# A six-layer cross network on one core: later loads, output copy, biases and first copies in another order, first tail weights loaded once

## The chip, the core and the metric

The kernel runs on one core of one Trainium2 chip. The metric is the device time of one execution in microseconds (us). The kernel before took 129.0 us (median of 3 runs, 128.87 to 129.28).

The engines are named as in the profile: PE (TensorE, matrix products, with its weight loads as PEld), DVE (VectorE), ACT (ScalarE), POOL (GpSimd) and SP (SyncE, which here only issues DMAs). ACT issues a few DMAs too. SBUF is the on-chip memory with 128 partitions, PSUM the banks into which PE writes.

## The reference

```python
B, F, D, L = 4096, 26, 16, 6          # Din = F * D = 416
x0: (4096, 416) bf16    ws: (6, 416, 416) bf16    bs: (6, 416) bf16

def reference(x0, ws, bs):
    x = x0
    for l in range(ws.shape[0]):
        x = x0 * (x @ ws[l] + bs[l]) + x
    return x
```

Every layer multiplies the current rows with a 416x416 matrix, adds a bias, multiplies by the first input elementwise and adds the current rows.

## The kernel before

**Form of the computation.** x after a layer is x0 times a sum, and the sum grows by one product and one bias per layer. So the sum stays in PSUM: PE adds each layer's product to it, and a layer ends when DVE adds the bias sum (`cb`) to the bank and multiplies by x0 (`leave`, L419). The bias sums of all layers are made once by `bias_sums` (L512): 16 small matmuls of `bsa_sb` (a row of ones, then the six bias rows; 7 partitions) with a 0/1 matrix `u_sb` (L265), copied to `cb_sb` by ACT.

**Tiling.** The 4096 rows are worked in NS = 4 blocks (s) of 1024 rows, each in two halves (h) of 512. Everything is held transposed, features in partitions: 416 = 3 chunks of 128 (c, k, m) and a tail of 32. The tails of the four groups of 256 rows lie in four quarters of 32 partitions (`quad(q)`). So the weights' tail rows `wt_sb` (32 rows of a layer) are wanted in all four quarters: `load_tail_weights` (L199) loads them four times from memory, once for each quarter, "wt0" for layer 0, "wt1" for layer 1, "wt2" for the rest. `corner` (L272, POOL) copies the last 32 columns of it into `wc_sb`.

**A layer (s, l).** On PE: the main products of half 0 (`main`, L312), then the tail rows for both halves (`tail_rows`, L328, in two functions `first` and `second`), then the tail's output columns (`tail_outs`, L370), then the main products of half 1. DVE leaves each bank. For the tail, ACT takes the two tail banks out of PSUM (`tail_halves`, L432), POOL multiplies by x0's tail (`leave_tail`, L441, the product at L449), and ACT and POOL make a swapped copy with two partition-shifted copies each (`swap`, L407, POOL's at L415). The next layer's tail rows wait for them. After each block but the last, `transpose_block` (L463) has SP issue three DMA transposes of the output chunks ("oT", L466) and one of the output tails ("ot", L471). `store_block` (L475) has POOL copy the transposed tails from `ot_sb` into `o_sb` (L477) and SP store the 1024 rows (L483); it is called for block s-1 in layer l = 1 of block s.

**Loads of x0.** The first half of block 0 comes as rows (`xin`, 2 x 208 KB, one on SP and one on ACT) and is transposed by PE (L497) into banks `HEAD_BANKS` and copied to `x0T_sb` by DVE (L506), six copies in the order (0,0), (1,0), (2,0), (0,1), (1,1), (2,1) of (chunk, part). All else comes by DMA transposes on SP: `load_transposed` (L203), and for the tails `load_last_columns` (L209), then `place_tail` (L215), six DMA copies within SBUF that wait for it. Block 0's tail comes from `xin` and `xtl` through PE (`tail_in`, L387) and ACT (L402).

**What sets the order.** `Plan.add` records each operation with what it reads and writes; each engine runs its operations in the order in which they were added, and waits are derived from the keys. `writes` replaces a key's writers, `parts` adds to them, `adds` is for accumulation. A POOL operation that shifts partitions (`shifts=True`) carries a key "shift". A queue's DMAs are issued in its engine's order too, so what waits on SP or ACT holds all that was added later.

In block 0, layer 0, PE's order is: `fill` (14 dummy matmuls, L285), the transposes, main products for k = 0, `bias_sums`, k = 1, `tail_in`, k = 2, `tail_rows`, `tail_outs`, half 1. The initial order of the DMA queues is at L229 to L249: SP issues xin0, three loads of layer 0's weights, the second half of block 0 transposed (x0T, L236), w1, wt1, w2, wt2, w3, w4, w5, and then for s = 1, 2, 3 the transposed loads, with `place_tail(1)` after block 1's, and last `xr` (the rows of block 3, for the end). ACT issues xin1, xtl, bs and the four copies of wt0.

The last layer of the last block is computed with rows in partitions (from L591) and is not touched.

Of the kernel before, what the change touches and what calls it, by code (L numbers as in the profile page):

```python
# [15 lines left out]
class Plan:  # L16
# [11 lines left out]
    def add(self, eng, fn, reads=(), writes=(), adds=(), parts=(), dma=None, shifts=False):  # L28
        if eng == "gpsimd" and dma is None:
            if shifts:  # L30
                adds = tuple(adds) + (("shift",),)
            else:
                reads = tuple(reads) + (("shift",),)
        op = Op()
        op.eng, op.fn, op.marked, op.dma, op.waits = eng, fn, False, dma, []
        needs = []
        for key in tuple(reads) + tuple(adds):
            needs += [(w, True) for w in self.writer.get(key, ())]
            if key[0] == "ps":
                needs += [(r, False) for r in self.readers.get(key, ())]  # L40
        for key in tuple(writes) + tuple(adds):
            needs += [(w, True) for w in self.writer.get(key, ())]
            needs += [(r, False) for r in self.readers.get(key, ())]
        for key in parts:
            needs += [(r, False) for r in self.readers.get(key, ())]
        clock = self.clock[eng]
        for need, raw in sorted(needs, key=lambda n: -n[0].idx):
            lane = need.group if need.dma else need.eng
            if dma and need.dma == dma:
                continue  # L50
            if need.dma is None and need.eng == eng and dma is None and (eng == "tensor" or not raw):
                continue
            if clock.get(lane, -1) >= need.idx:
                continue
            op.waits.append(need)
            need.marked = True
            for lane2, idx in need.clock.items():
                clock[lane2] = max(clock.get(lane2, -1), idx)
            clock[lane] = max(clock.get(lane, -1), need.idx)
        op.idx = len(self.ops[eng])  # L60
        op.group = None
        if dma:
            op.group = ("dma", dma)
            members = self.groups.setdefault(op.group, [])
            members.append(op)
            op.marked = True
        op.clock = dict(clock)
        self.ops[eng].append(op)
        for key in reads:
            self.readers.setdefault(key, []).append(op)  # L70
        for key in parts:
            if self.readers.get(key):
                self.writer[key], self.readers[key] = [], []
            self.writer.setdefault(key, []).append(op)
        for key in tuple(writes) + tuple(adds):
            old = self.writer.get(key, ())
            keep = [w for w in old if dma and w.dma == dma]
            self.writer[key] = keep + [op]
            if not keep:
                self.readers[key] = []  # L80
        return op
# [37 lines left out]
def bass_standalone__dcn_v2_cross__recsys_kernel(  # L119
# [6 lines left out]
    B, D = x0.shape  # L126
# [15 lines left out]
    with ExitStack() as es:  # L142

        def sb(name, shape, dt=BF16):
            return es.enter_context(nc.sbuf_tensor(name, shape, dt))
# [20 lines left out]
        ident = sb("ident", [128, 128])  # L166
        ones_sb = sb("ones_sb", [128, 128])
        dummy_sb = sb("dummy_sb", [128, 8])
        bsa_sb = sb("bsa_sb", [L + 1, D])
        u_sb = sb("u_sb", [L + 1, L])  # L170
        cb_sb = sb("cb_sb", [128, NC + 1, L], FP32)
        bt_sb = sb("bt_sb", [128, 1], FP32)
        ps = es.enter_context(nc.psum_tensor("ps", [128, 8, 512], FP32))
# [56 lines left out]
        load_rows("scalar", 1)  # L230
        for k in CH:
            load("sync", w_sb[:, 0, k, :], ws[0, 128 * k:128 * k + 128, :], "w0_%d" % k, [("w", 0, k)])
        load("scalar", xtl_sb[:, 4:JS, :], x0_v[:, 4:JS, DF:D], "xtl0", [("xtl", 0)])
        load("scalar", bsa_sb[1:L + 1, :], bs[:, :], "bs", [("bs",)])
        load_tail_weights(0, 1, "wt0", "scalar")
        load_transposed(0, H, SB)  # L236
        load_main(1)
        load_tail_weights(1, 2, "wt1")
# [2 lines left out]
        load_main(3)  # L241
        load_main(4)
        load_main(5)
        for s in range(1, NS):
            load_transposed(s, 0, SB)
            load_last_columns(s)
            if s == 1:
                place_tail(1)
        load("sync", xr_sb[:, :, :], x0_v[:, (NS - 1) * JS:NJ, :], "xr", [("xr",)])  # L249


        P.add("vector", lambda e: e.memset(ones_sb[:, :], 1.0), writes=[("ones",)])
# [7 lines left out]
                compare_op=ALU.is_equal, fill=0.0, base=0, channel_multiplier=1,  # L260
            ), reads=[("ones",)], writes=[("ident",)],
        )
        P.add("gpsimd", lambda e: e.memset(bsa_sb[0:1, :], 1.0), writes=[("bs1",)])
        P.add(
            "gpsimd", lambda e: e.affine_select(  # L265
                out=u_sb[:, :], in_=ones_sb[0:L + 1, 0:L], pattern=[[1, L]],
                compare_op=ALU.is_ge, fill=0.0, base=1, channel_multiplier=-1,
            ), reads=[("ones",)], writes=[("u",)],
        )
        P.add("gpsimd", lambda e: e.memset(wc_sb[:, :, :], 0.0), writes=[("wc", "wt%d" % i) for i in range(3)])  # L270

        def corner(a, b, name):  # L272
            P.add(
# [217 lines left out]
        for i in range(2):  # L491
            for c in CH:
                b = HEAD_BANKS[i][c]

                def fn(pe, i=i, c=c, b=b):
                    for j in range(2):
                        ins = pe.transpose(  # L497
                            out=psT[:, b, j * 128:(j + 1) * 128],
                            in_=xin_sb[:, 2 * i + j, c * 128:(c + 1) * 128], identity=ident[:, :],
                        )  # L500
                    return ins

                P.add("tensor", fn, reads=[("xin", i), ("ident",)], adds=[("ps", b)])
                dst, src = x0T_sb[:, c, i * 256:(i + 1) * 256], psT[:, b, 0:256]
                P.add(
                    "vector", lambda e, d=dst, s=src: e.tensor_copy(out=d, in_=s),  # L506
                    reads=[("ps", b)], writes=[("x0Tp", c, i)],
                )
        for c in CH:
            P.writer[("x0T", 0, c, 0)] = [w for i in range(2) for w in P.writer[("x0Tp", c, i)]]  # L510

# [17 lines left out]
            )  # L529


        corner(0, 1, "wt0")
        for s in range(NS):
            for l in range(L):
                ending = s == NS - 1 and l == L - 2
                if s == NS - 1 and l == L - 1:
                    break
                if s == 0 and l == 0:
                    for k in CH:
                        for part in range(2) if k == 0 else (None,):  # L540
                            for m in CH:
                                main(s, l, 0, m, k, part)
                        if k == 0:
                            bias_sums()
                        if k == 1:
                            tail_in()
                    tail_rows(s, l, True)
                    for c in CH:
                        leave(s, l, 0, c)
                    tail_outs(s, l, False)  # L550
                else:
                    for m in CH:
                        for k in CH:
                            main(s, l, 0, m, k)
                    tail_rows(s, l, l == 0)
                    for c in CH:
                        leave(s, l, 0, c)
                    tail_outs(s, l, False)
                if s == 0 and l == 1:
                    corner(2, L, "wt2")  # L560
                leave_tail(s, l, not ending)
                if l == 2 and 0 < s < NS - 1:
                    place_tail(s + 1)
                if s == 0 and l == 0:
                    corner(1, 2, "wt1")
                if l == 1 and s > 0:
                    store_block(s - 1)
                if ending:
                    P.add(
                        "gpsimd", lambda e: e.tensor_tensor(  # L570
                            out=bt_sb[:, :], in0=cb_sb[:, NC, L - 1:L], in1=cb_sb[:, NC, L - 2:L - 1], op=ALU.subtract
                        ), reads=[("cb",)], writes=[("bt",)],
                    )
                    P.add(
                        "gpsimd", lambda e, t=t32_sb[:, l % 2, :]: e.tensor_scalar_add(st_sb[:, :], t, bt_sb[:, :]),
                        reads=[("t32", l % 2), ("bt",)], writes=[("st",)],
                    )
                    for c in CH:
                        keep_sum(0, c, "scalar")
                for m in CH:  # L580
                    for k in CH:
                        main(s, l, 1, m, k)
                    leave(s, l, 1, m)
                if ending:
                    for c in CH:
                        keep_sum(1, c, ("scalar", "scalar", "vector")[c])
            if s < NS - 1:
                transpose_block(s)


        s, l = NS - 1, L - 1  # L591
# [128 lines left out]
```

## Time and profile before

| | us |
|---|---|
| runs, median of 3 | 129.0 (128.87 to 129.28) |
| profiled execution | 130.0 |
| its span, first to last instruction | 128.5 |
| PE busy | 123.2 |
| DVE busy | 98.5 |
| ACT busy | 43.5 |
| POOL busy | 37.4 |
| first main matmul, first tail matmul of layer 0 | 4.62, 8.52 |
| last matmul issued | 125.5 |

The granted PE clock was full (1.0) throughout. Matmuls are pipelined, and their ends are modelled, so a row's busy time is not its cost; what a stage costs is read from the starts of the same row in consecutive layers. "Idle before, releaser" in a row is how long the engine stood still before it and what ended that.

### The profile page before, as it was taken

What the parts mean: (1) busy time and instruction counts of PE and PEld (TensorE: products, weight loads), DVE (VectorE), ACT (ScalarE), POOL (GpSimd) and SP (SyncE); (2) the same over time, 40 slices, a digit from 0 to 9 for tenths busy, and PEclk for the clock granted to TensorE, in tenths of its full rate; (3) what the DMA queues carried; (4) which work ended last, traced back from release to release, by engine and by line L of the source; (5) the groups of instructions that cost most, each with busy time, mean ns of one, the idle gap of its engine ahead of it and who ended that gap; (6) DMA issues with size and microseconds to landing.
All of it is one profiled execution on the core that took longest, in us unless ns stands there. A gap on an engine that the chain in (4) does not pass through costs nothing.

```text
span 128.5 us, 5300 instructions
## 1 busy us (share of the span) xinstructions
PE 123.2 (96%) x2414; PEld 64.3 (50%) x2414; DVE 98.5 (77%) x152; ACT 43.5 (34%) x95; POOL 37.4 (29%) x79
## 2 busy tenths in 40 slices
PE   7979999999999999799999999999999999999991
PEld 5544554555545545345545545545555455455660
DVE  0329779779779779497797797797797797797973
ACT  0515225225205222343222252252222252253920
POOL 6005224134014040442221251241320351440550
PEclk9999999999999999999999999999999999999999
DMA  3998999013989894630009207200007706100017
GB/s 102 231 255 223 295 83 211 5 32 82 220 146 192 215 275 85 216 98 5 0 6 204 66 0 247 67 5 0 5 0 176 94 5 219 51 0 5 0 38 232
DMA packets 35059, 14.11 MB, mean 110 GB/s; under 512 B 25751, under 2 KB 35037, under 8 KB 35037
## 3 DMA queue, kind: packets, MB, share of 16 engines
q1 hardware_dynamic: 33744, 13.20, 48.5%
q10 hardware_dynamic: 1292, 0.57, 1.7%
q8 instruction: 19, 0.31, 1.1%
q14 instruction: 4, 0.02, 0.1%
HBM read 3.87 MB, written 3.41 MB: 57 GB/s over the span
## 4 chain that ended last, share of the span: by engine, by line
PE 83%; DMA 6%; DVE 4%; ACTq 2%; POOL 1%; issue 1%; SPq 0%
PE ps L280 83%; DMA wt_sb<-in_ws_dram 4%; DVE xT_sb L426 3%; DMA ot_sb<-xot_sb 3%; ACTq L189 2%; POOL xt_sb L415 1%; POOL xt_sb L449 0%; DVE o_sb L651 0%; SPq L466 0%; POOL o_sb L477 0%
## 5 line engine op out<-in xcount | busy, mean ns | idle before, releaser
L426 DVE SCALAR_TENSOR_TENSOR xT_sb<-ps,cb_sb,x0T_sb 128x512 bf16<-128x512 f32 x120 | 80.9, 743 | 20.2 <-PE ps L280 20.2
L280 PE MATMUL ps<-xT_sb,w_sb 128*32 128x512 bf16 (+1 forms) x1596 | 84.2, 364 | 0.0
L280 PEld LDWEIGHTS ps<-xT_sb,w_sb 128*32 128x32 bf16 x1596 | 40.9, 97 | 37.2 <-issue 4.0
L436 ACT ACTIVATE t_sb<-ps,cb_sb 64x256 f32<-64x256 f32 x46 | 21.6, 470 | 56.7 <-PE ps L280 56.4
L449 POOL TENSOR_TENSOR xt_sb<-t_sb,x0t_sb 128x256 bf16<-128x256 f32 x20 | 13.4, 672 | 59.2 <-ACT t_sb L436 59.2
L413 ACT ACTIVATE xt_sb<-xt_sb 32x256 bf16<-32x256 bf16 x38 | 15.7, 414 | 17.0 <-POOL xt_sb L449 16.7
L280 PE MATMUL ps<-x0T_sb,w_sb 128*32 128x512 bf16 (+1 forms) x348 | 18.8, 358 | 0.3 <-DVE x0T_sb L506 0.3
L415 POOL COPY xt_sb<-xt_sb 32x256 bf16<-32x256 bf16 x38 | 14.9, 393 | 2.4
L426 DVE SCALAR_TENSOR_TENSOR xo_sb<-ps,cb_sb,x0T_sb 128x512 bf16<-128x512 f32 x18 | 12.1, 742 | 2.5 <-PE ps L280 2.5
L280 PEld LDWEIGHTS ps<-x0T_sb,w_sb 128*32 128x32 bf16 x348 | 8.6, 97 | 7.8 <-issue 0.8
L280 PE MATMUL ps<-xt_sb,wt_sb 32*128 32x512 bf16 (+1 forms) x152 | 11.6, 326 | 0.8 <-POOL xt_sb L415 0.8
L280 PE MATMUL ps<-xt_sb,wc_sb 32*128 32x256 bf16 x76 | 7.3, 268 | 0.0
L280 PEld LDWEIGHTS ps<-xt_sb,wt_sb 32*128 32x128 bf16 x152 | 2.4, 91 | 8.9 <-DVE xT_sb L426 6.8
L280 PE MATMUL ps<-w_sb,xT_sb 128*32 128x416 bf16 (+1 forms) x60 | 5.1, 339 | 0.0
L449 POOL TENSOR_TENSOR xot_sb<-t_sb,x0t_sb 128x256 bf16<-128x256 f32 x3 | 2.0, 672 | 9.9 <-ACT t_sb L436 9.9
L651 DVE TENSOR_TENSOR o_sb<-ps,xr_sb 128x416 bf16<-128x416 f32 x6 | 3.4, 588 | 1.3 <-PE ps L280 1.0
L280 PEld LDWEIGHTS ps<-xt_sb,wc_sb 32*128 32x128 bf16 x76 | 3.9, 93 | 0.2
L288 PE MATMUL ps<-const-bfloat16-1.0 128*128 128x256 bf16 x14 | 3.1, 414 | 0.8 <-PEq L705 0.8
L506 DVE COPY x0T_sb<-ps 128x256 bf16<-128x256 bf16 x6 | 1.3, 282 | 3.1 <-PE ps L497 3.1
L280 PE MATMUL ps<-x0t_sb,wt_sb 32*128 32x512 bf16 (+1 forms) x32 | 2.4, 325 | 0.8 <-DMA wt_sb<-in_ws_dram 0.8
L458 ACT ACTIVATE sS_sb<-ps,cb_sb 128x512 bf16<-128x512 f32 x5 | 3.0, 691 | 0.0
L274 POOL COPY wc_sb<-wt_sb 128x32 bf16<-128x32 bf16 (+1 forms) x3 | 0.7, 237 | 7.7 <-DMA wt_sb<-in_ws_dram 7.6
(38 smaller groups left out, 26.7 us busy)
## 6 DMA issues: line engine op xcount, KB each, us to landing
out_dram<-o_sb SPq DMA_DIRECT2D x3, 832.0 KB, 4.2
w_sb<-in_ws_dram SPq DMA_DIRECT2D x5, 312.0 KB, 5.1
xr_sb<-in_x_dram SPq DMA_DIRECT2D x1, 832.0 KB, 6.4
wt_sb<-in_ws_dram SPq DMA_DIRECT2D x4, 104.0 KB, 3.5
out_dram<-o_sb SPq DMA_DIRECT2D x2, 208.0 KB, 2.2
w_sb<-in_ws_dram SPq DMA_DIRECT2D x3, 104.0 KB, 3.3
xin_sb<-in_x_dram ACTq DMA_DIRECT2D x1, 208.0 KB, 3.2
xin_sb<-in_x_dram SPq DMA_DIRECT2D x1, 208.0 KB, 3.0
```

The lines of the kernel that those rows point to most:

```text
L189: P.add(queue, lambda e: e.dma_start(dst, src), writes=writes, dma=name)
L274: "gpsimd", lambda e: e.tensor_copy(out=wc_sb[:, a:b, 3 * DR:4 * DR], in_=wt_sb[:, a:b, DF:D]),
L280: return pe.matmul(dst, lhsT=lhsT, rhs=rhs, start=start, stop=True, skip_group_check=True, tile_position=pos,)
L288: ins = pe.matmul(ps[:, 7, 0:256], lhsT=const[:, 0:128], rhs=const, start=True, stop=True)
L413: fn = lambda e, d=dst, s=src: e.activation(out=d, in_=s, func=ACTF.Copy)
L415: fn = lambda e, d=dst, s=src: e.tensor_copy(out=d, in_=s)
L426: "vector", lambda e: e.scalar_tensor_tensor(out=dst, in0=ps[:, bank(h, c), :], scalar=cb_sb[:, c, l:l + 1], in1=x0T_sb[:, c, o:o + H], op ...
L436: "scalar", lambda e, p=p, h=h: e.activation(out=dst[p, :], in_=ps[p, T_BANK[h], 0:G], func=ACTF.Identity, bias=cb_sb[p, NC, l:l + 1]), re ...
L449: "gpsimd", lambda e: e.tensor_tensor(out=dst, in0=t, in1=x0t_sb[:, s, 0, :], op=ALU.mult),
L458: fn = lambda e: e.activation(out=o, in_=i, func=ACTF.Identity, bias=b)
L506: "vector", lambda e, d=dst, s=src: e.tensor_copy(out=d, in_=s),
L651: "vector", lambda e: e.tensor_tensor(out=o_sb[:, jj, :], in0=ps[:, b, 0:D], in1=xr_sb[:, j, :], op=ALU.mult), reads=[("ps", b), ("xr",)], ...
```

## The change

Six edits:

1. wt0, the tail weights of layer 0, are loaded once, into the first quarter, as ACT's second DMA (before xtl). A new function `replicate`, called just before the first `corner`, copies them to the other quarters: to 1 and 2 by POOL, to 3 by ACT.
2. bs is loaded by a DMA that POOL issues, after DVE has cleared the whole of `bsa_sb`; DVE also writes the row of ones, which POOL did. `bsa_sb` and `u_sb` now have 128 partitions instead of 7.
3. `bias_sums` stands behind `tail_in` (after k = 1) instead of after k = 0.
4. DVE's six first copies are taken out of the transposes' loop and stand in the order (0,0), (1,0), (0,1), (2,0), (1,1), (2,1).
5. The transposed loads of blocks 2 and 3 and `xr` are no longer issued at the start, but behind the output transposes of blocks 0, 1 and 2.
6. `store_block(s-1)` is called in layer 3 of block s instead of layer 1.

One line in `Plan.add` makes a shifting POOL operation wait for the end of the POOL operations ahead of it, which before were only in order.

```diff
-            needs += [(r, False) for r in self.readers.get(key, ())]
+            needs += [(r, key == ("shift",)) for r in self.readers.get(key, ())]
...
-        bsa_sb = sb("bsa_sb", [L + 1, D])
-        u_sb = sb("u_sb", [L + 1, L])
+        bsa_sb = sb("bsa_sb", [128, D])
+        u_sb = sb("u_sb", [128, L])
...
+        load("scalar", wt_sb[quad(0), 0, :], ws[0, DF:D, :], "wt0", [("wtq",)])
         load("scalar", xtl_sb[:, 4:JS, :], x0_v[:, 4:JS, DF:D], "xtl0", [("xtl", 0)])
-        load("scalar", bsa_sb[1:L + 1, :], bs[:, :], "bs", [("bs",)])
-        load_tail_weights(0, 1, "wt0", "scalar")
...
-        for s in range(1, NS):
-            load_transposed(s, 0, SB)
-            load_last_columns(s)
-            if s == 1:
-                place_tail(1)
-        load("sync", xr_sb[:, :, :], x0_v[:, (NS - 1) * JS:NJ, :], "xr", [("xr",)])
+        load_transposed(1, 0, SB)
+        load_last_columns(1)
+        place_tail(1)
...
-        P.add("gpsimd", lambda e: e.memset(bsa_sb[0:1, :], 1.0), writes=[("bs1",)])
+        P.add("vector", lambda e: e.memset(bsa_sb[:, :], 0.0), writes=[("bs0",)])
+        P.add("vector", lambda e: e.memset(bsa_sb[0:1, :], 1.0), reads=[("bs0",)], writes=[("bs1",)])
+        P.add("gpsimd", lambda e: e.dma_start(bsa_sb[1:L + 1, :], bs[:, :]), reads=[("bs0",)], writes=[("bs",)], dma="bs")
...
+        def replicate():
+            for g, eng in ((1, "gpsimd"), (3, "scalar"), (2, "gpsimd")):
+                dst, src = wt_sb[quad(g), 0, :], wt_sb[quad(0), 0, :]
+                if eng == "scalar":
+                    fn = lambda e, d=dst, r=src: e.activation(out=d, in_=r, func=ACTF.Copy)
+                else:
+                    fn = lambda e, d=dst, r=src: e.tensor_copy(out=d, in_=r)
+                P.add(eng, fn, reads=[("wtq",)], parts=[("wt", "wt0")], shifts=True)
...
+        for c, i in ((0, 0), (1, 0), (0, 1), (2, 0), (1, 1), (2, 1)):
+            dst, src = x0T_sb[:, c, i * 256:(i + 1) * 256], psT[:, HEAD_BANKS[i][c], 0:256]
...
+        replicate()
         corner(0, 1, "wt0")
...
-                        if k == 0:
-                            bias_sums()
                         if k == 1:
                             tail_in()
+                            bias_sums()
...
-                if l == 1 and s > 0:
+                if l == 3 and s > 0:
                     store_block(s - 1)
...
             if s < NS - 1:
                 transpose_block(s)
+            if s < NS - 2:
+                load_transposed(s + 2, 0, SB)
+                load_last_columns(s + 2)
+            if s == NS - 2:
+                load("sync", xr_sb[:, :, :], x0_v[:, (NS - 1) * JS:NJ, :], "xr", [("xr",)])
```

More of the change, by code (lines that the diff above doesn't have):

```diff
@@ L262, in bass_standalone__dcn_v2_cross__recsys_kernel @@
         )
-        P.add("gpsimd", lambda e: e.memset(bsa_sb[0:1, :], 1.0), writes=[("bs1",)])
+        P.add("vector", lambda e: e.memset(bsa_sb[:, :], 0.0), writes=[("bs0",)])
+        P.add("vector", lambda e: e.memset(bsa_sb[0:1, :], 1.0), reads=[("bs0",)], writes=[("bs1",)])
+        P.add("gpsimd", lambda e: e.dma_start(bsa_sb[1:L + 1, :], bs[:, :]), reads=[("bs0",)], writes=[("bs",)], dma="bs")
         P.add(
             "gpsimd", lambda e: e.affine_select(
-                out=u_sb[:, :], in_=ones_sb[0:L + 1, 0:L], pattern=[[1, L]],
+                out=u_sb[:, :], in_=ones_sb[:, 0:L], pattern=[[1, L]],
                 compare_op=ALU.is_ge, fill=0.0, base=1, channel_multiplier=-1,
@@ L503, in bass_standalone__dcn_v2_cross__recsys_kernel @@
                 P.add("tensor", fn, reads=[("xin", i), ("ident",)], adds=[("ps", b)])
[L504 to L508, printed above, removed]
+        for c, i in ((0, 0), (1, 0), (0, 1), (2, 0), (1, 1), (2, 1)):
+            dst, src = x0T_sb[:, c, i * 256:(i + 1) * 256], psT[:, HEAD_BANKS[i][c], 0:256]
+            P.add(
+                "vector", lambda e, d=dst, s=src: e.tensor_copy(out=d, in_=s),
+                reads=[("ps", HEAD_BANKS[i][c])], writes=[("x0Tp", c, i)],
+            )
         for c in CH:
```

## The prediction

> **What bounds the kernel now.** I read the page's busy shares first, then the chain that ended last in order of time, then TensorE's instructions in order of time, then the waits and the DMA landings. The page, of the kernel before:
>
> ```profile
> span 128.5 us, 5300 instructions
> PE 123.2 (96%) x2414; PEld 64.3 (50%) x2414; DVE 98.5 (77%) x152; ACT 43.5 (34%) x95; POOL 37.4 (29%) x79
> ```
>
> TensorE is busy almost throughout, so only time in which TensorE stands still can be won. The chain in order of time (start, length, what) says where that is:
>
> ```profile
> 3.84 4.55 DMA wt_sb<-in_ws_dram
> 8.39 0.14 issue
> 8.52 34.59 PE ps L280 x648
> ...
> 47.81 3.31 DMA ot_sb<-xot_sb
> 51.12 0.05 issue
> 51.17 0.40 POOL o_sb L477
> 51.56 0.64 POOL xt_sb L449
> 52.21 0.05 issue
> 52.26 0.40 POOL xt_sb L415
> 52.66 0.05 issue
> 52.71 0.41 POOL xt_sb L415
> 53.12 0.14 issue
> 53.25 72.61 PE ps L280 x1388
> ```
>
> The reader is to see two foreign pieces between long TensorE pieces: the last of four loads of the first layer's tail weights, landing at 8.39, and a transpose of the output's tail (ot) for which GpSimd waits until 51.12. TensorE's own list shows what the second costs; these are the first tail matmuls of consecutive layers:
>
> ```profile
> 42.67 0.60 PE L280 MATMUL ps<-xt_sb,wt_sb 32*128 32x512 bf16 x7
> ...
> 47.55 0.60 PE L280 MATMUL ps<-xt_sb,wt_sb 32*128 32x512 bf16 x7
> ...
> 53.25 0.59 PE L280 MATMUL ps<-xt_sb,wt_sb 32*128 32x512 bf16 x7 [0.76 <-POOL xt_sb L415]
> ...
> 58.13 0.60 PE L280 MATMUL ps<-xt_sb,wt_sb 32*128 32x512 bf16 x7
> ```
>
> The step is 4.88 us from layer to layer (42.67 to 47.55, 53.25 to 58.13), but 5.70 from 47.55 to 53.25: 0.82 us lost. All other steps from 8.52 to 116.67 are 4.88, so nothing else stalls there.
>
> **The output copy, -0.82.** store_block(0) stands in layer l=1 of the next block; its copy (L477) heads GpSimd's queue and waits for ot:
>
> ```profile
> POOL o_sb L477 <- DMA ot_sb<-xot_sb: 4.8, 1, 4.8
> ```
>
> Queued behind it are the tail product (L449) and two swaps (L415), for which TensorE waits. The change moves the copy to l=3, about 10 us later, behind that layer's swaps. There it takes its 0.40 us (L477, 397 ns) out of GpSimd's idle stretch before the next product, 3.29 us in an ordinary layer (before 44.82). Without that cover it would cost at most 0.40 less the 1.15 us between the end of the swaps (41.52) and TensorE's need (42.67): nothing. Blocks 1 and 2 had no such wait (the row counts one), so the gain comes once. I take 0.82.
>
> On SP's queue the loads for blocks 2 and 3 and xr no longer stand ahead of block 0's output transposes: issues of 3.25 + 1.30 + 4.60 + 1.30 + 1.51 = 11.96 us (29.53 to 41.66). Before, oT0 was issued only at 41.70, though the DVE had its last tile by about 37.5; so ot should now land near 43, long before any copy asks. The price is later loads. x0T of block 2 would be issued near 41.5 and land 7.5 us later (the median of the four) near 49, for matmuls that begin at 65.84; its place_tail (six issues, 4.9 us) still ends before 60, for a use at 67.89. Block 3's come behind oT1 and ot1, which end at 71.49: land by about 80, x0t by 88, needed at 95 and 97. xr is issued near 101 behind ot2 and lands 6.4 us later, needed after 121. The output of block 0 leaves behind place_tail(2), that of block 2 about 114, landing 4.2 us later. Covers of 7 us and more: cost nothing.
>
> **The head.** Today first tail matmuls start at 8.52, 0.13 after the last wt0 landing; tail_outs start at 9.07. ScalarE issues wt0 as its fourth to seventh DMA (2.54 to 4.28). After the change one 26 KB copy is issued second, at about 1.30, where xtl stood, which landed 3.3 us later: at about 4.6. Then:
>
> - ScalarE no longer issues bs (0.66) and three wt0 (0.32 to 0.44 each), so its table load starts near 2.3, not 4.31; it is free at 3.8. Its 32x416 copy is bounded by a 32x256 copy (414 ns) and a 128x512 one (598): 0.53, done at 5.2, far from x0t at 6.9. Its tail input xtl is issued 0.45 later, lands near 5.1, needed at 6.5.
> - GpSimd does ident (to 1.42), the bs DMA (X), u (0.18), the clearing of wc (1.21), two copies, the corner (0.21). The copy goes by L415 (32x256, 393 ns) and L274 (128x32, 210 ns): 0.82 ns an element, so 0.52 at 416. With 0.1 for gaps the copies end at 1.42 + X + 0.18 + 1.21 + 1.04 + 0.10 = 3.95 + X. No row shows a DMA issued by GpSimd. [...] I take 0.66: done at 4.6, then held by wt0's landing to about 5.8.
> - The DVE's new clearing of bsa (like the 0.17 of L252) and the ones row (0.43 on GpSimd) end by 1.7; the DVE is idle to 4.17. Its reordered copies gain nothing: TensorE's pause at 5.31 is for bank 2, which holds the copy of (1,1), fifth in both orders.
> - bias_sums now follow tail_in. Their 16 matmuls (0.19 of TensorE's time, 5.86 to 6.05) change places, so k=2 starts at 6.93 as before and ends 0.64 later, 7.57; tail_in comes 0.19 earlier, so ScalarE's x0t ends at 7.57, not 7.76. With 128 rows in place of 7, weight loads may add 0.17 (x16 of 128x32 took 0.34, of 7x32 0.17), hidden by what follows.
>
> So tail matmuls could start at 7.65 and tail_outs 0.55 later, at 8.20, 0.87 before today. But tail_outs also read the transposed second half of block 0:
>
> ```profile
> x0T_sb<-in_x_dram SPq DMA_TRANSPOSE x1, 5.9
> ```
>
> Issued at 2.75, it lands at about 8.62. This is late next: 8.62 + 0.13 = 8.75. It may land sooner, since three of the four wt0 copies, 78 KB, leave the same engines; between 4.60 and 7.50 they carried 191 GB/s, so at most 0.42, at least 0. I take half, 0.21: tail_outs at 8.54, a gain of 0.53, with ends 0.32 and 0.87. The second layer's weights w1, issued at 4.88 and landing 4.5 later (9.4), are in time for 10.8.
>
> **Sum:** -0.82 - 0.53 = -1.35. The profiled execution took 130.0 us, its span 128.5, with 1.5 around it; the changed one should show a span of 127.1 and 128.6 in all. The runs' median, 129.0, is 1.0 below the profiled execution; the same difference gives 127.7.
>
> **Rivals.**
>
> *Only the GpSimd stall goes.* bs or the copies are late by just as much as wt0 was, or x0T binds later. For it: X and the landing of bs are in no row. Against it: bs is needed at 6.74, 5.3 us after its issue, and the loads issued in the first 4 us took 3.0 to 4.7, the transpose 5.9. Time: 129.0 - 0.82 = 128.2.
>
> *Only the head gains.* Executions without the profiler are 1.0 us shorter; if ot lands earlier in them, the stall is not there to be won. For it is that difference; against it, SP's loads ahead of ot fill its queue in any execution. 129.0 - 0.53 = 128.5.
>
> *Slower: GpSimd is held by its DMA.* Place: what stands behind bs in its queue, the wc clearing and the weight copies, for which the first tail matmuls wait. They start at 3.95 + X. Up to X = 4.0 it costs nothing (tail_outs wait for x0T until 8.54); at 4.57 the head's gain is gone; at 8.52 + 0.82 - 3.95 = 5.39 the whole gain. With the 6.99 of the longest issue row they start at 10.94, 2.42 late: 129.0 + 2.42 - 0.82 = 130.6. Against it: that row carries 1024 rows to transpose, bs six short ones.
>
> *Slower, by the bias wait.* If GpSimd's descriptors are not written before the DVE's six copies end (5.45) and bs needs xtl's 3.3 from there, it lands at 8.75; bias sums (0.13 + 0.19) and k=2 (0.64) put tail matmuls at 9.71, 1.19 late: 129.0 + 1.19 - 0.82 = 129.4. Against it: the DVE is idle from about 1.7 to 4.17, when GpSimd needs it to be. The Trainium skill ("SBUF — State Buffer", section "SBUF: two separate sides") has the rule behind this: a DMA issued by GpSimd has its descriptors written by GpSimd, which is locked out while the DVE runs a two-port fast mode. No row of this trace shows it.
>
> A fixed cost for DMAs issued by GpSimd stands in the Trainium skill ("DMA: Bandwidth & Descriptors", section "Anatomy of one DMA — SWDGE (gpsimd) path"): about 2.0 us, mostly completion. As an estimate by it bs would be there near 3.7, and the sum stays. No row here has it.
>
> **How the numbers follow.** Forecast 0.65; stall alone 0.14; head alone 0.10; GpSimd held 0.07; bias wait 0.04. A measurement of this kernel tells a difference from none at about 0.3%, 0.39 us: faster means below 128.6. The forecast and the stall alone are there, the head alone (128.5) so close to the bound that I give half of it: 0.84 faster; the other 0.05 and 0.02 for a GpSimd held by 5.0 to 5.8 make 0.07 the same; the rest, 0.09, is slower (X above 5.39 + 0.39 = 5.78, or the bias wait). The forecast's own range is 129.0 - 0.82 - 0.87 = 127.3 to 127.9 with the low gain; 0.3 below for what the x0T landing may add; up to 128.6 to hold both half gains: 127.0 to 128.6.
>
> **What would show it.** Right: layer steps of 4.88 throughout, with no wait of L477's copy; first tail matmuls near 7.7, then TensorE idle for x0T until about 8.5. Wrong: a TensorE wait for bs or for GpSimd's weight copies before the first tails, a GpSimd DMA of over 4 us, or a new wait for x0T, x0t or xr at 65, 95 or 121.

## The result, and the profile after

| | before | changed |
|---|---|---|
| median, us | 129.28 (15 runs, 128.87 to 129.97) | 128.62 (15 runs, 128.31 to 129.20) |
| ratio | | 0.9953, interval 0.9936 to 0.9971 |
| profiled execution, its span | 130.0, 128.5 | 129.03, 127.5 |

The change is faster: by 0.66 us of the medians (0.51%), by 0.47% in the ratio of the runs. The forecast was 127.7, a gain of 1.35 from a median of 129.0; the direction is right, the size about half, and the time lies just above the range. The kernel before took 129.28 in these 15 runs, so 0.28 of the distance to 127.7 lies in the median that the forecast set out from. The profiled executions differ by more than the medians, by 1.0: the 130.0 of the kernel before lies above all its 15 runs here, the 129.03 within those of the changed kernel. The page of the changed kernel begins:

```profile
span 127.5 us, 5305 instructions
PE 123.9 (97%) x2414; PEld 65.0 (51%) x2414; DVE 99.2 (78%) x154; ACT 44.0 (35%) x96; POOL 39.0 (31%) x81
```

Its chain that ended last, in order of time:

```profile
...
0.83 3.15 PE ps L295 x14
3.98 1.41 PE ps L504 x12
5.39 2.88 PE ps L287 x68
8.27 0.05 issue
8.32 116.51 PE ps L287 x2216
...
```

Both foreign pieces are gone: the chain is TensorE from the first dummy matmul on. TensorE's rows in order of time show the layers where the stall was:

```profile
47.34 0.60 PE L287 MATMUL ps<-xt_sb,wt_sb 32*128 32x512 bf16 x7
...
52.22 0.60 PE L287 MATMUL ps<-xt_sb,wt_sb 32*128 32x512 bf16 x7
...
57.10 0.60 PE L287 MATMUL ps<-xt_sb,wt_sb 32*128 32x512 bf16 x7
```

The steps are 4.88, and so are all others up to the last layer's at 115.64. The profiles thus differ by 0.82 in the stall and by only 0.20 in the head: the first tail matmuls went from 8.52 to 8.32, not to 7.65. Why shows in the timeline of the head. The kernel before:

```profile
3.81 0.89 PE L497 MATMUL ps<-ident,xin_sb 128*128 128x128 bf16 x12
...
7.16 0.60 ACT L402 ACTIVATE x0t_sb<-ps 128x512 bf16<-128x512 f32 x1 [0.77 <-PE ps L280]
...
8.52 0.59 PE L280 MATMUL ps<-x0t_sb,wt_sb 32*128 32x512 bf16 x7 [0.77 <-DMA wt_sb<-in_ws_dram]
```

The changed kernel:

```profile
1.58 0.75 POOL L261 DMA_DIRECT2D bsa_sb<-in_bs_dram  x1 [0.15 <-issue]
...
3.93 1.46 PE L504 MATMUL ps<-ident,xin_sb 128*128 128x128 bf16 x12
...
4.98 1.11 POOL L276 COPY wt_sb<-wt_sb 32x416 bf16<-32x416 bf16 x2 [1.27 <-DMA wt_sb<-in_ws_dram]
...
7.58 0.60 ACT L409 ACTIVATE x0t_sb<-ps 128x512 bf16<-128x512 f32 x1 [2.16 <-PE ps L287]
...
8.32 0.59 PE L287 MATMUL ps<-x0t_sb,wt_sb 32*128 32x512 bf16 x7
```

The same twelve transposes took 0.89 us in one execution and 1.46 in the other, a step of 0.055 against 0.106 us: TensorE ran at half speed in the second. The first full-speed record of the granted clock stands at 3.93 in the trace of before and at 6.37 in that of the changed kernel. Most executions of the kernel before hardly feel this, since its head ends with a DMA (in a2 below, which has the same head, the two stand level at a clock of 5.95); the head of the changed one is paced by TensorE.

### The profile page after: what moved, and what is told of

Same layout as the page of the kernel before. It is cut to its first block, busy times and chain, and to the rows that moved or that the text cites. A ratio compares the mean times of both kernels' runs of the same rounds, so it can differ in the third digit from the quotient of the medians.

```text
span 127.5 us, 5305 instructions
## 1 busy us (share of the span) xinstructions
PE 123.9 (97%) x2414; PEld 65.0 (51%) x2414; DVE 99.2 (78%) x154; ACT 44.0 (35%) x96; POOL 39.0 (31%) x81
## 4 chain that ended last, share of the span: by engine, by line
PE 97%; DVE 0%; issue 0%
PE ps L287 94%; PE ps L295 2%; PE ps L504 1%; DVE o_sb L664 0%
## 5 line engine op out<-in xcount | busy, mean ns | idle before, releaser
L287 PEld LDWEIGHTS ps<-w_sb,xT_sb 128*32 128x32 bf16 (+1 forms) x60 | 2.3, 97 | 1.4 <-issue 0.2
L675 POOL TENSOR_TENSOR o_sb<-f_sb,xr_sb 128x416 bf16<-128x416 f32 x2 | 1.9, 974 | 2.9 <-ACT f_sb L671 2.9
```

What stands on the lines that cost most here:

```text
L287: return pe.matmul(dst, lhsT=lhsT, rhs=rhs, start=start, stop=True, skip_group_check=True, tile_position=pos,)
L675: "gpsimd", lambda e: e.tensor_tensor(out=o_sb[:, jj, :], in0=t, in1=xr_sb[:, j, :], op=ALU.mult),
```

## The experiments

Ratios are to the kernel before on the same chip. In the table of heads (one profile each, us), "clock" is the first full-speed record of the granted clock in the trace (that of d2 holds none), "wt0" the last landing of the tail weights, "x0t" the end of ScalarE's copy, "k=2" the start of TensorE's last products before the tails, "x0T" the landing of block 0's second half, "tails" the first tail matmul.

| kernel | ratio | clock | wt0 | x0t | k=2 | x0T | tails |
|---|---|---|---|---|---|---|---|
| before, first profile | | 3.93 | 8.39 | 7.75 | 6.93 | 8.62 | 8.52 |
| a1 before again | 1.0016 | 5.51 | 8.31 | 7.98 | 7.16 | 8.52 | 8.44 |
| a2 edit 6 alone | 0.9985 | 5.95 | 8.18 | 8.20 | 7.37 | 8.40 | 8.32 |
| a4 edits 5, 6 | 0.9983 | 5.47 | 8.22 | 7.96 | 7.14 | 8.45 | 8.36 |
| changed, first profile | 0.9953 | 6.37 | 4.84 | 8.17 | 7.46 | 7.86 | 8.32 |
| b1 changed again | 0.9953 | 5.01 | 4.58 | 7.75 | 7.04 | 7.53 | 7.90 |
| d4 changed again | 0.9946 | 5.43 | 4.69 | 7.84 | 7.12 | 7.80 | 7.98 |
| a3 edits 1 to 4 | 0.9927 | 4.52 | 4.48 | 7.67 | 6.95 | 7.52 | 7.81 |
| b2 edits 1 to 4 again | 0.9971 | 5.79 | 4.88 | 7.91 | 7.19 | 7.70 | 8.05 |
| c1 edit 1 alone | 0.9989 | 5.53 | 4.49 | 8.37 | 7.55 | 7.67 | 8.43 |
| c2 without edit 1 | 0.9948 | 3.88 | 7.94 | 7.44 | 6.96 | 8.17 | 8.07 |
| c3 tail_in earlier | 0.9943 | 5.68 | 6.05 | 7.24 | 7.05 | 7.45 | 7.80 |
| c4 bs on ScalarE | 0.9933 | 4.93 | 4.57 | 7.75 | 7.03 | 7.25 | 7.80 |
| d1 c3 and c4 | 0.9935 | 4.95 | 5.46 | 7.12 | 7.05 | 7.35 | 7.80 |
| b3 changed, 1 dummy | 1.0052 | 8.84 | 4.67 | 9.06 | 8.35 | 7.70 | 9.32 |
| b4 before, 1 dummy | 1.0036 | 9.11 | 8.06 | 9.41 | 8.55 | 8.24 | 9.57 |
| d2 edit 5 alone | 0.9978 | | 8.36 | 7.89 | 7.07 | 8.56 | 8.50 |
| d3 copy in layer 0 | 1.0506 | 4.06 | 8.13 | 7.84 | 7.02 | 8.32 | 8.27 |

### The kernel before again, and the parts of the change alone

No edit in a1:

> The kernel before, unchanged, profiled a second time. Theory A (the GpSimd stall of 0.82 us is in every execution, and the head of the changed kernel gives part of it back): this profile again has a step of 5.70 us from the second to the third layer of block 1, and the tail weights land near 8.4. Theory B (the stall of the first profile was one execution's; most executions lose 0.3 us or less there): that step is at most 5.2 us, and the span is nearer 127.8 than 128.5. Clock theory (the clock of TensorE rises at a time that differs from execution to execution): the twelve transposes take 0.9 us here or 1.5 us, and in this kernel the first tail matmuls start at 8.4 to 8.6 either way, since they wait for a DMA. Ratio 1.000 within 0.002.

Its timeline shows the place of the stall without a stall:

```profile
47.47 0.60 PE L280 MATMUL ps<-xt_sb,wt_sb 32*128 32x512 bf16 x7
...
49.44 0.40 POOL L477 COPY o_sb<-ot_sb 128x256 bf16<-128x256 bf16 x1 [3.12 <-DMA ot_sb<-xot_sb]
49.80 0.67 POOL L449 TENSOR_TENSOR xt_sb<-t_sb,x0t_sb 128x256 bf16<-128x256 f32 x1
...
52.35 0.60 PE L280 MATMUL ps<-xt_sb,wt_sb 32*128 32x512 bf16 x7
```

ot landed at 49.39, not at 51.12, and TensorE's step is 4.88. GpSimd still waits 3.12 us, but hidden. The expected clock difference is there too: transposes 1.48 us, tails at 8.44, 0.13 behind the landing of wt0 (8.31). That is theory B's case; one profile does not say how often it comes, and six are counted below. Ratio 1.0016 (0.9993 to 1.0040). The profiled execution took 129.16, a little less than the median of a1's runs (129.34), so profiling does not by itself lengthen an execution: the 130.0 was a long one among its kind.

```diff
# a2_store
-                if l == 1 and s > 0:
+                if l == 3 and s > 0:
                     store_block(s - 1)
# a4_late: the same, with edit 5 of the change
# a3_head, b2_head: edits 1 to 4 of the change
```

> Edit 6 alone: the copy and store of a finished block in layer 3 of the next block, all else as before. Theory A: 0.82 us faster, ratio 0.9937. Theory B: 0.1 to 0.3 us faster, ratio 0.998 to 0.999. Both: all steps 4.88 us from the first tail matmuls on.

> Edits 5 and 6 alone: later loads behind the output transposes and the copy in layer 3, the head as before. Both theories: the same as edit 6 alone, since the moved loads have 7 us and more of cover; theory A 0.82 us faster (0.9937), theory B 0.1 to 0.3 us faster (0.998 to 0.999).

Measured: a2 0.9985 (0.9960 to 1.0011), a4 0.9983 (0.9966 to 1.0001), so 0.2 us, with intervals that reach no gain. The 0.9937 of theory A lies outside both. The spread says little: a1's runs reach from 128.85 to 130.35 and those of a4 only to 129.35, but one run of a2 took 130.20.

> Edits 1 to 4 alone: the head as in the changed kernel, the later loads and the output copy as before. Theory A: no gain or slightly slower, ratio 0.999 to 1.002. Theory B: 0.3 to 0.6 us faster, ratio 0.995 to 0.998. Clock theory: first tail matmuls between 7.6 and 8.5, later where the transposes take 1.5 us than where they take 0.9.

> Edits 1 to 4 alone, again. Clock theory: a spread of 0.6 us or more once there are enough executions, ratio 0.992 to 0.996, and its single GpSimd stall in the executions where ot lands late. Rival: ratio 0.993 and better than the whole change.

a3 came out at 0.9927 (0.9907 to 0.9946), better than theories A and B had it, b2, the same kernel, at 0.9971 (0.9952 to 0.9990), less good than its clock theory and its rival had it. The two intervals do not meet: two measurements of one kernel, on two chips, lie 0.0044 apart, so smaller differences between ratios are not told apart here by one measurement each. The profile of b2 has a stall again, by its timeline:

```profile
47.08 0.60 PE L290 MATMUL ps<-xt_sb,wt_sb 32*128 32x512 bf16 x7
...
50.49 0.40 POOL L487 COPY o_sb<-ot_sb 128x256 bf16<-128x256 bf16 x1 [4.57 <-DMA ot_sb<-xot_sb]
...
52.58 0.59 PE L290 MATMUL ps<-xt_sb,wt_sb 32*128 32x512 bf16 x7 [0.56 <-POOL xt_sb L425]
```

Here the step is 5.50, 0.62 over 4.88. The tail matmuls start 2.09 us after GpSimd's copy (50.49 to 52.58). In the first profile it was 2.08 (51.17 to 53.25). In a1 49.44 + 2.09 is 51.53, ahead of the due 52.35: no stall. In c1 the copy at 50.42 gives 52.51 against a due 47.45 + 4.88 = 52.33, and its step was 5.05, 0.17 more than 4.88. So the price is the landing of ot plus 2.1 us, less the due time.

Six profiled executions leave the loads and the copy where the kernel before has them (the first profile, a1, a3, b2, b4, c1). Their steps lose 0.82, 0, 0, 0.62, 0.17 and 0 us, 0.27 in the mean, which is what the runs without the stall won. ot landed at 51.12, 49.39, 48.17, 50.44, 50.37 and 49.02. SP came to issue it at 47.81 in the first profile and at 45.43 in a1; it was already 3 us later at block 1's `place_tail` (24.73 against 21.75). What makes its queue run late in one execution is not shown.

### The price of the late output transpose

```diff
# d3_copy_l0
-                if l == 1 and s > 0:
+                if l == 0 and s > 0:
                     store_block(s - 1)
# d2_loads: edit 5 of the change alone, the copy stays in layer 1
```

> Edit 5 alone: the later loads behind the output transposes, the copy still in layer 1, the head as before. Theory (the price of the stall is the lateness of ot): ot lands near 43 as in the changed kernel, GpSimd's copy has no wait, no step over 4.88; the same gain as the moved copy, ratio 0.997 to 0.999. Rival: a gain of 0.82 us, 0.9937, or none.

> The kernel before with the copy one layer earlier still, in layer 0. Theory: GpSimd asks at about 41.5 and waits for ot until 49.4 to 51.1; the product due at 44.8 starts 5.0 to 6.8 us late, of which 1.15 are slack; the step from the first to the second layer of block 1 is 8.7 to 10.5 instead of 4.88, other blocks lose at most 0.5; 3.9 to 5.7 us slower, ratio 1.030 to 1.045. Rival (the wait is mostly hidden, and the 0.82 of the first profile came from something else): under 1 us slower.

d2: ot landed at 43.66, all steps 4.88, ratio 0.9978 (0.9963 to 0.9992). GpSimd's copy, still in layer 1, starts at 46.50, 2.84 us after that landing; in a2 it starts at 56.08, 6.08 after ot (50.00). So either edit alone takes the stall away, and the ratios of a2, a4 and d2 are not told apart. d3: 1.0506 (1.0449 to 1.0563), more than expected. Its TensorE rows and, below, three windows (us, then busy time and instructions of each engine, granted clock, DMA share, GB/s):

```profile
42.42 0.60 PE L280 MATMUL ps<-xt_sb,wt_sb 32*128 32x512 bf16 x7
52.77 1.01 PE L280 MATMUL ps<-xt_sb,wt_sb 32*128 32x512 bf16 x7 [5.41 <-POOL xt_sb L415]
60.48 0.60 PE L280 MATMUL ps<-xt_sb,wt_sb 32*128 32x512 bf16 x7
```

```profile
46.00:51.80 5.80, 1.36 (x28) 0.43 (x18) 0.93 (x2) 0.04 (x1) 1.04 (x3) 1.00 0.99 129
51.90:58.60 6.70, 5.83 (x64) 2.50 (x68) 3.70 (x6) 2.45 (x6) 2.12 (x5) 0.50 0.47 148
58.70:64.00 5.30, 5.30 (x112) 2.65 (x108) 3.58 (x6) 1.59 (x4) 1.25 (x3) 1.00 0.01 3
```

The stall itself is as expected: a step of 10.36 us, 5.48 over 4.88, and the tails again 2.07 after the copy (50.70). But TensorE stood for 5.41 us, its clock fell to half until 58.7, and the next step took 7.71, 2.83 more. That second part was in neither theory. It differs between executions: of the six runs, four with a mean granted clock of 0.975 took 136.99 to 138.02 us, two with 0.987 took 135.29 and 135.45.

### What ends the head

```diff
# b3_after_cold (in the changed kernel), b4_before_cold (in the kernel before)
-        fill(14)
+        fill(1)
```

> The changed kernel again, beside its head edits alone. Clock theory: its head is paced by TensorE, whose clock rises between about 3.9 and 7 us at a time that differs between executions; so the executions spread over 0.9 us, the profile's first tail matmuls stand at 7.8 if the clock rises at 4.5, at 8.3 if at 6.4, and the ratio is the same as that of the head edits alone less 0.001 to 0.002: 0.990 to 0.994. Rival (the moved loads or the later copy cost in the whole kernel what the head wins): ratio 0.995 again, 0.002 to 0.003 worse than the head alone on the same chip.

> The changed kernel with 1 dummy matmul at the start in place of 14, so that TensorE is not busy before the transposes and its clock rises later. Clock theory: transposes at 0.106 us a step, main products at half speed, first tail matmuls near 9.4 to 9.8, 1.2 to 2.5 us slower than the changed kernel (ratio to the kernel before 1.005 to 1.015). Rival (landings set the head): first tails at 8.3 or earlier, ratio as without the edit.

> The kernel before with 1 dummy matmul in place of 14. Clock theory: first tail matmuls near 9.4 to 9.8, as in the changed kernel with the same edit, 0.9 to 1.8 us slower than the kernel before (ratio 1.007 to 1.015): both heads are then paced by TensorE, and the change's gain in the head is gone. Rival: first tails stay at 8.4 to 8.5, the landing of the tail weights, ratio 1.000.

b1: 0.9953 (0.9935 to 0.9970), tails at 7.90 with the clock at 5.01, as the clock theory had it; the ratio is less good than its 0.990 to 0.994, and is what the rival expected against a3, but better than b2's beside it on the same chip (0.9971, with an interval that overlaps): a cost of the late edits is not shown. With one dummy matmul the clock rose only near 9. b3: 1.0052 (1.0028 to 1.0076), tails at 9.32, a little earlier than expected; b4: 1.0036 (1.0011 to 1.0062), less slow than expected, tails at 9.57. Now x0t is the later of the two in the kernel before as well (9.41, wt0 8.06): once the clock is late enough, both heads are TensorE's. By the runs the gain of the change is gone, though in the two profiles, with clocks at 8.84 and 9.11, its tails still stand 0.25 earlier.

```diff
# c1_wt0: the kernel before with edit 1 alone (and the line in Plan.add)
# c2_four: the changed kernel, wt0 by load_tail_weights(0, 1, "wt0", "scalar") behind xtl, no replicate()
# c3_tailin: the changed kernel, xtl issued ahead of wt0, and
-                        if k == 1:
+                        if k == 0:
                             tail_in()
+                        if k == 1:
                             bias_sums()
# c4_bs_act: the changed kernel, bs on ScalarE's queue behind xtl
# d1_both: c3 and c4 together
```

> The kernel before with edit 1 alone: the tail weights loaded once and copied by GpSimd and ScalarE. Theory (in the kernel before the head ends with the landing of the fourth tail weight load, in the changed one with TensorE's pace, tail_in and ScalarE's x0t copy): first tail matmuls 0.15 us after the x0t copy ends, 7.9 to 8.5 by the clock; x0T's second half lands near 7.7, not 8.5; ratio 0.995 to 0.999. Rival (the order of bias sums and first copies matters as much): no change, first tails at 8.4.

> The changed kernel without edit 1: four loads of the tail weights again, behind xtl. Theory: first tails again wait for the fourth landing at 8.0 to 8.3, since bs no longer stands ahead of them on ScalarE's queue, and stand at 8.2 to 8.5; what is left of the gain is the late part and 0.1 to 0.2 of the head: ratio 0.996 to 0.999. Rival: first tails 0.15 us after x0t, ratio 0.995 as the whole change.

c1: 0.9989 (0.9962 to 1.0016), so a gain of edit 1 alone is not shown. Without the fourfold load wt0 is there at 4.49 and x0T at 7.67, but the x0t copy ends at 8.37 and becomes the end of the head: 8.43. a1, with the same order of work and nearly the same clock (5.51 against 5.53), had x0t at 7.98. The 0.39 between them is a new wait. In c1 bs is ScalarE's fourth DMA, issued at 2.33 behind wt0 and xtl (in the kernel before its third, at 1.85), and bias_sums, still ahead of k = 1, start at 6.48 instead of 6.09:

```profile
6.48 0.26 PE L289 MATMUL ps<-u_sb,bsa_sb 7*32 7x6 bf16 x16 [0.31 <-DMA bsa_sb<-in_bs_dram]
```

So edit 1 leans on edit 3, which puts the sums behind tail_in: c4 below, with bs on that queue again but the sums there, has no such wait. c2: 0.9948 (0.9924 to 0.9972), the ratio of the rival: the runs do not show that edit 1 adds anything to the rest. Its profile has the theory's wait, though earlier than the 8.2 to 8.5 expected. With a clock that rose at 3.88 its tails still waited, by its timeline:

```profile
8.07 0.64 PE L287 MATMUL ps<-x0t_sb,wt_sb 32*128 32x512 bf16 x7 [0.28 <-DMA wt_sb<-in_ws_dram]
```

wt0 landed at 7.94 (bs no longer stands ahead of it), x0t was ready at 7.44. So each part removes one of two late events (wt0 and x0t stood 0.64 apart in the first profile, 0.33 in a1, 0.02 in a2), and the head moves only as far as the other.

> The changed kernel with xtl loaded ahead of the tail weights and tail_in ahead of k=1 instead of behind it. Theory: the x0t copy ends 0.6 us earlier and no longer holds the first tails, which start where TensorE's k=2 products end, 0.1 to 0.2 us earlier than in the changed kernel at the same clock: ratio 0.993 to 0.995, at best 0.002 better than the changed kernel. Rival (the copies of the tail weights hold the first tails): no earlier start.

> The changed kernel with bs loaded by ScalarE's queue behind xtl instead of by GpSimd. Theory: GpSimd's DMA (0.75 us of its time, landing near 6.0, needed at 6.9) was hidden, so nothing changes: ratio 0.994 to 0.997, as the whole change. Rival (the GpSimd DMA costs in executions without its luck): 0.002 or more better.

> The changed kernel with xtl ahead of the tail weights, tail_in ahead of k=1, and bs on ScalarE's queue. Theory: the head ends where TensorE's products end, first tails at 7.6 to 7.9 by the clock; ratio 0.992 to 0.995, 0.001 to 0.002 better than the changed kernel beside it. Rival: the same as the changed kernel within 0.001.

> The changed kernel a third time, beside d1_both. Clock theory: ratio 0.994 to 0.996, first tails between 7.8 and 8.4 by the time at which the clock rises.

c3: 0.9943 (0.9918 to 0.9968). Its tails stand at 7.80 with the clock at 5.68, earlier than those of d4 at 5.43; its timeline shows what ends the head there:

```profile
3.77 1.49 PE L504 MATMUL ps<-ident,xin_sb 128*128 128x128 bf16 x12
...
6.64 0.60 ACT L409 ACTIVATE x0t_sb<-ps 128x512 bf16<-128x512 f32 x1
...
7.05 0.81 PE L287 MATMUL ps<-x0T_sb,w_sb 128*32 128x512 bf16 x12
...
7.80 0.60 PE L287 MATMUL ps<-x0t_sb,wt_sb 32*128 32x512 bf16 x7
```

x0t is ready at 7.24; the tails follow TensorE's own k=2 products. These start at 7.05 and end, by an estimate, about 0.68 later (36 such products took 2.05 in the first profile, 35.74 to 37.79), at 7.73. c4: 0.9933 (0.9907 to 0.9960); d1: 0.9935 (0.9911 to 0.9959); d4, the changed kernel beside d1: 0.9946 (0.9925 to 0.9968). The intervals overlap widely: that c4 or d1 beats the changed kernel is not shown. What bs through GpSimd costs, if anything, is too small for these runs, and the profiles show no wait for it: in the changed kernel's three it landed between 5.99 and 6.20, and the bias sums began at 6.93 or later.

## Why the prediction was wrong in size

- **The output copy, -0.82: the step that failed.** The mechanism was right (GpSimd's queue, ot, the chain behind it; 2.07 to 2.09 us from copy to tails in the four profiles with a stall), the size was not. In place of 0.82 the runs without the stall won 0.15 to 0.22% (a2, a4, d2), about 0.2 to 0.3 us, and the six profiles with it lost 0.27 in the mean. Each of these ratios alone is near the limit of what is told apart, but the 0.9937 of a full 0.82 lies outside all three intervals. The term was read from one execution, in which ot landed at 51.12; in a1, the same kernel, it landed at 49.39 and in b4 at 49.02, where the wait is hidden. The prediction then took 0.82 off a median that held only a part of it. Its own rival "only the head gains" (128.5, chance 0.10) had the reason, an ot that lands earlier in other executions, and came closest to the 128.62; its guess that the profiler makes the difference is not borne out, since a1's profiled execution took 129.16.
- **The later loads** cost nothing, as said: block 2's x0T landed at 48.31 and its x0t at 55.17, block 3's at 76.77 and 83.70, xr at 105.11 (forecast 49, 60, 80, 88, 107).
- **wt0 and its copies** came as worked out: landing at 4.84 (4.6), ScalarE's copy 0.55 (0.53), GpSimd's two 1.11 (1.04), done at 6.09 (5.8). GpSimd's DMA held it 0.75 (0.66 forecast, from ScalarE's row for the same load; the rival's 6.99 was SP's row for x0T at 12.26), and bs landed at 6.20, in time: both slower rivals fell. The loads with which the prediction compared bs took 2.8 to 4.8 us by their rows, not 3.0 to 4.7, which changes nothing. xtl, issued behind wt0, was mis-sized: it landed at 6.24 to 6.76 in the three profiles, not at 5.1, and only 0.31 to 0.47 before tail_in began, so it stayed hidden. The Trainium skill ("DMA: Bandwidth & Descriptors", section "Anatomy of one DMA — SWDGE (gpsimd) path") has a fixed cost of about 2.0 us for such a DMA; here issue to landing was 4.6 us, beside other loads (a DMA share of 1.15 and 1.20 between 3.90 and 6.40).
- **x0T's landing as the next limit** was wrong: it came at 7.53 to 7.86 in the changed kernel (8.41 forecast), before TensorE wanted it in every profile. Taking away three of four wt0 loads gained about 0.8 on it, not 0.21, and more than the 0.42 that was to be the most: with four loads it landed at 8.17 to 8.62 (eight profiles, median 8.43), with one at 7.25 to 7.86 (ten, median 7.60; c1, with edit 1 alone, 7.67). What stood in its place was TensorE's pace: k=2 began at 7.04 to 7.46, not at 6.93, and x0t ended at 7.75 to 8.17, not at 7.57, because the first profile of before had the full clock from 3.93 and I took its rows as the speed of the head. c2, whose clock rose at 3.88, has the forecast's pace: k=2 at 6.96, x0t at 7.44. So the first tails came at 7.90 to 8.32, not at 7.65, and TensorE did not then stand idle for x0T. The two errors nearly cancel, which is luck: tail_outs stand at 8.87, 8.45 and 8.53 in the three profiles, forecast 8.54.
- **The head, -0.53:** against tail_outs at 9.07 and 8.99 in the two profiles of before, the median of the three above (8.53) is 0.46 to 0.54 less. With 0.2 to 0.3 for the copy this makes about the 0.66 measured. The head edits by themselves measured 0.73% and 0.29% (a3, b2), too far apart to size them better.
- That DVE's new copy order gains nothing was not tried by itself and stays open. Nor were edits 2 and 3 tried without the rest.

## What to carry to other kernels

A stall seen once in a profile may be a race between a DMA's landing and a due time: before its price is taken off a median, ask whether the profiled execution is slower than the runs, and by how much, and profile the unchanged kernel again. Where a wait is removed from a start-up phase, list all that arrives within half a microsecond of it, TensorE's own pace at half clock among it, and take rows for that pace from an execution with a late clock too.

## What the runs showed of the hardware

- In kernels with 14 dummy matmuls the clock of TensorE rose between 3.88 and 6.37 us (15 traces; that of d2 has no record), in the same program at 5.01, 5.43 and 6.37; with one dummy matmul at 8.84 and 9.11. Transposes stepped 0.055 us with it and 0.106 without. The Trainium skill ("TensorE: Matmul & The Clock Gate", section "Part 1: The HAM clock gate (the "warmup" mystery)") says why it may vary: the activity window is free-running and does not start with the kernel. That the time moves agrees; the section gives about 0.5 us either way, and here the spread is 2.5 us. No run here could set the phase.
- The clock column of the profile showed 1.00 in these first microseconds even where the steps had doubled, since the trace's clock record begins at the rise. So the full clock said of the kernel before holds only from 3.93 on: its dummy matmuls of 256 columns started 0.213 us apart, the pace of 0.106 for 128.
- In d3, in mid-kernel, the column showed 0.50 from 51.84 to 58.67, after TensorE had stood still since 47.36 (5.41 us in all), and that half clock cost 2.83 us more: in the profiled execution a stall of 5.5 us had a price of 8.3.
